# A chunked recurrence's output made by channel: two heads on two column halves, three full channel tiles, and masked products that alternate between row halves

## The chip, the cores and the metric

One core of a Trainium2 chip. Times are device microseconds of one launch, the median of three or more runs. All arithmetic is float32. In the profile of this kernel a float32 product is two instructions on TensorE (PE): RV's eight products in each of 24 chunks count 384. So "x16" is eight products.

## The reference, cut to what matters

```python
batch, n_heads, seq, head_dim = (4, 8, 768, 40)
for t in range(S):
    y[:, :, t] = np.einsum('bhd,bhde->bhe', rt, state)
    Sa = np.einsum('bhde,bhe->bhd', state, at)
    state_decay = state * wt[:, :, None, :] - np.einsum('bhd,bhe->bhde', Sa, bt)
    state = state_decay + np.einsum('bhd,bhe->bhde', vt, kt)
# ... y as (batch * seq, 320), then
h = np.maximum(x @ w_in, 0.0)          # w_in 320 x 2048
return (h * h @ w_out)                 # w_out 2048 x 320
```

## The kernel before

The recurrence runs in chunks of 128 steps: 4 batches with 6 chunks each are 24 chunks. Within a chunk the eight heads go in four pairs. A head has 40 channels, padded to 64, so a pair fills 128 partitions. Everything that depends on the state is a handful of products per head; the inverse of a triangular matrix (six levels of products and transposes) takes the largest part of TensorE's time (27.5 of 70.3 us in a regular chunk, by start-to-start distances). After every two chunks the second part, the squared-relu network, gets 256 tokens. Its blocks of six `w_in` or eight `w_out` instructions are issued between the stages of the recurrence, so that TensorE has work while DVE or ACT empties PSUM (below: evicts a block).

Four places matter. The masked products, one row half (parity of the head) after the other:

```python
def products(name, bufs, l_, r_):
    res = []
    for e in range(2):
        p_ = quads(psum(ps_w))
        rows = slice(e * DP, e * DP + D)
        for q in range(NP):
            mm(p_[:, q], l_[rows, q, :], r_[rows, q, :], True)
        # ... DVE multiplies by the triangular mask
```

They make N, A, RV and RX: 4 x 24 = 96 blocks of 16 instructions. The output of a chunk, by token, with 40 streamed columns for each head:

```python
heads(y_, g["RV"], lambda h: k_[:, h, :D], True)
for q in range(NP):
    mm(y_[:, 2 * q:2 * q + 2], rT[:, q], sd[:, q, :, :D], False)
heads(y_, rx, lambda h: b_[:, h, :D], False)
nc.vector.tensor_tensor(ys, y_, g["wn"], Alu.mult)     # wn: the decays, turned back to tokens
```

The turning of the tokens to channels, and the second part, whose 320 channels are tiles of 128, 128 and 64 rows:

```python
for j, (o, m_) in enumerate(KT):
    nc.tensor.transpose(p_[:m_, j * C:(j + 1) * C], ys[:, o:o + m_], ident)
# ... copies by ACT, then
for j, (_, m_) in enumerate(KT):
    mm(p_, w_in[:m_, j, f * 128:(f + 1) * 128], t_[:m_, j, :], j == 0)
```

Of the kernel before, what the change touches and what calls it, by code (L numbers as in the profile page):

```python
# [17 lines left out]
def kernel(  # L18
# [11 lines left out]
):  # L30
    # The recurrence runs in chunks of C steps.  Within a chunk, with E_j the product of the decays
    # of the steps before j and all products taken relative to the middle of the chunk:
    #   a' = a E_t, k' = k / E_t+1, b' = b / E_t+1           (per key channel)
    #   N = strictly lower (a' b'^T), A = strictly lower (a' k'^T)
    #   x = (I + N)^-1 (a' S^T + A v)                         (the rows S a of all steps)
    #   y = E_t (r S + low(r v^T) k' - low(r x^T) b')
    #   S <- E_C (S + v^T k' - x^T b')
    # (I + N)^-1 is exact: the inverses of its diagonal blocks, doubled in size level by level.
    # Heads go in pairs, 64 partitions or columns each; tiles by head are [., parity, pair, .].
    nc = tc.nc  # L40
# [10 lines left out]
    GB = 2  # L51
    KT = [(o, min(128, DM - o)) for o in range(0, DM, 128)]

# [13 lines left out]
    def single(name, shape):  # L67
        return const.tile(shape, FP32, tag=name, name=name)
# [5 lines left out]

# [1 line left out]
    class Ring:  # L76
# [19 lines left out]
    def load(i):  # L96
        bb, c = order[i]
        loaded[i] = {}
        for nm, ring in rings.items():
# [4 lines left out]

# [1 line left out]
    ident = single("ident", [128, 128])  # L106
# [6 lines left out]
                            pattern=[[1, 128]], channel_multiplier=-1)  # L113
    # -1 at [2p, 2p + 1]: the first level, transposed.
    first = single("first", [128, 128])
# [4 lines left out]
                            pattern=[[-2, 64]], channel_multiplier=1)  # L120
    # -1 where the row is in the second and the column in the first half of one block of 2 n.
    halves = {}
    for lv in range(1, LEVELS):
# [9 lines left out]
                                pattern=[[2 * n, count], [0, n]], channel_multiplier=-1)  # L133
    # 1 where a state's row and column belong to the same head of a pair.
    same = single("same", [128, NP, 2])
# [7 lines left out]

    w_in = single("w_in", [128, len(KT), DFF])
    w_out = single("w_out", [128, NF, DM])

    # Weights come as float64 in raw words: the chip rounds them to float32.  hi holds the sign, 11 bits
    # of exponent and 20 of mantissa, lo the 32 bits below.  With p = sign and power of two, from hi:
    # weight = (p with hi's mantissa) + p lo 2^-52, the sum rounded once.
    def rounded(dst, src, n):  # L150
        raw = work.tile([128, WP, 2], I32, tag="raw", name="raw")[:n, :dst.shape[-1]]
        nc.scalar.dma_start(out=raw.rearrange("p f e -> p (f e)"), in_=src.bitcast(I32))
        lo, hi = raw[:, :, 0].bitcast(U32), raw[:, :, 1]
        power = work.tile([128, WP], I32, tag="power", name="power", bufs=1)[:n, :dst.shape[-1]]
        p_ = work.tile([128, WP], I32, tag="signed", name="signed", bufs=1)[:n, :dst.shape[-1]]
        bits = dst.bitcast(I32)
        nc.vector.tensor_scalar(power, hi, 20, 0x7FF, Alu.logical_shift_right, Alu.bitwise_and)
        nc.vector.tensor_scalar(power, power, 896.0, 1151.0, Alu.max, Alu.min)
        nc.vector.tensor_scalar(power, power, 896.0, float(1 << 23), Alu.subtract, Alu.mult)
        nc.vector.tensor_scalar(p_, hi, -(1 << 31), None, Alu.bitwise_and)  # L160
        nc.vector.tensor_tensor(p_, p_, power, Alu.bitwise_or)  # L161
        nc.vector.tensor_scalar(bits, hi, 0xFFFFF, 3, Alu.bitwise_and, Alu.logical_shift_left)
        nc.vector.tensor_tensor(bits, bits, p_, Alu.bitwise_or)  # L163
        rest = power.bitcast(FP32)
        nc.vector.scalar_tensor_tensor(rest, lo, 2.0 ** -52, p_.bitcast(FP32), Alu.mult, Alu.mult)  # L165
        nc.vector.tensor_tensor(dst, dst, rest, Alu.add)

    WP = 320
    WI = 256
    pieces = [(w_in[:n, j, f:f + WI], moe_w_in[o:o + n, f:f + WI], n)  # L170
              for f in range(0, DFF, WI) for j, (o, n) in enumerate(KT)]
    pieces += [(w_out[:, f, :], moe_w_out[f * 128:(f + 1) * 128, :], 128) for f in range(NF)]

    def load_weights(n):
        for _ in range(min(n, len(pieces))):
            dst, src, rows = pieces.pop(0)
            if src.dtype == FP32:
                nc.scalar.dma_start(out=dst, in_=src)
            else:
                rounded(dst, src, rows)  # L180

# [1 line left out]
    def turn(x_):  # L183
# [5 lines left out]
    def products(name, bufs, l_, r_):  # L189
        """Strictly upper part of l_^T r_ by head, as one tile a parity."""  # L190
        res = []
        for e in range(2):
            p_ = quads(psum(ps_w))
            rows = slice(e * DP, e * DP + D)
            for q in range(NP):
                mm(p_[:, q], l_[rows, q, :], r_[rows, q, :], True)
            t_ = work.tile([128, NP, 128], FP32, tag=name, name=name, bufs=bufs)
            nc.vector.tensor_tensor(t_, p_, over4(upper), Alu.mult)  # L198
            res.append(t_)
        return res  # L200

    def inverse(g):
        """(I + N)^-1 transposed, from N transposed: both parities in step, a stage at a time."""
        new = lambda nm, bufs: work.tile([128, NP, 128], FP32, tag=nm, name=nm, bufs=bufs)
# [38 lines left out]
    def decay(i, g):  # L243
        """Products of the decays, and N, which the inverse waits for."""
        x_ = loaded[i]
# [18 lines left out]
    def rest(i, g):  # L264
        """What the chain needs beside the inverse."""
        x_ = loaded.pop(i)
        up, down, aT = g["dec"][:, 0], g["dec"][:, 1], g["aT"]
        kT, rT, vT = turned("kT", 1), turned("rT", 2), turned("vT", 1)
# [16 lines left out]

        wn = g["wn"] = work.tile([128, H, D], FP32, tag="wn", name="wn")
        nc.scalar.copy(wn, back(up[:, :, :C]))
        yield
        inv = back(down[:, :, 1:C + 1])
# [5 lines left out]

# [1 line left out]
    ended, tokens = {}, {}  # L297

    def chain(i, g):
# [53 lines left out]
        yield  # L353
        y_ = by_head(psum(ps_c))
        heads(y_, g["RV"], lambda h: k_[:, h, :D], True)
        if c > 0:
            for q in range(NP):
                mm(y_[:, 2 * q:2 * q + 2], rT[:, q], sd[:, q, :, :D], False)
        heads(y_, rx, lambda h: b_[:, h, :D], False)
        ys = work.tile([128, H, D], FP32, tag="ys", name="ys")  # L360
        nc.vector.tensor_tensor(ys, y_, g["wn"], Alu.mult)  # L361
        yield
        gather(i, ys.rearrange("t h d -> t (h d)"))
        yield

# [1 line left out]
    def gather(i, ys):  # L367
        """Tokens of GB chunks by channel, for the second part."""
        n = i % GB
        if n == 0:  # L370
            tokens[i // GB] = work.tile([128, len(KT), GB * C], FP32, tag="tokens", name="tokens")
        t_ = tokens[i // GB]
        p_ = psum(ps_c)
        for j, (o, m_) in enumerate(KT):
            nc.tensor.transpose(p_[:m_, j * C:(j + 1) * C], ys[:, o:o + m_], ident)  # L375
        full = sum(m_ == 128 for _, m_ in KT)
        nc.scalar.copy(t_[:, :full, n * C:(n + 1) * C], p_[:, :full * C].rearrange("p (j t) -> p j t", j=full))
        for j in range(full, len(KT)):
            m_ = KT[j][1]
            nc.scalar.copy(t_[:m_, j, n * C:(n + 1) * C], p_[:m_, j * C:(j + 1) * C])  # L380

    PART = NF // 4

    def ffn():
        for gi in range(len(order) // GB):
# [4 lines left out]
            for f in range(NF):  # L390
                p_ = psum(ps_f)[:, :GB * C]
                for j, (_, m_) in enumerate(KT):
                    mm(p_, w_in[:m_, j, f * 128:(f + 1) * 128], t_[:m_, j, :], j == 0)
                h_ = work.tile([128, GB * C], FP32, tag="hid", name="hid", bufs=NF + 2)
                nc.scalar.activation(h_, p_, Act.Relu)  # L395
                nc.vector.tensor_tensor(h_, h_, h_, Alu.mult)  # L396
                hid.append(h_)
                yield True
# [12 lines left out]

    # ---- in the order that the engines take it: while one stage's result leaves PSUM, the tensor
# [1 line left out]
    second = ffn()  # L414
# [70 lines left out]
```

## Time and profile before

| | before |
|---|---|
| median of three runs (lowest, highest) | 1795.6 us (1790.55, 1799.59) |
| mean granted clock of TensorE, profiled run | 0.970 |
| start of the fifth chunk (weights unpacked, second part running) | 293.8 us |
| regular chunk at full clock | 70.29 us |
| last chunk and the second part after it | 151.8 us |

The last three are read from the starts of TensorE's instructions: a chunk starts with the transpose of its `w`. Chunks alternate between 72.3 and 68.3 us, because every second one has more of the second part; 70.29 is the mean of twelve.

This is the table of windows again, cut where the stages change (columns: window, length, busy us of PE, PEld (its weight loads), DVE, ACT, POOL, then clock, DMA share, GB/s):

```profile
0.00:294.00 294.00, 237.11 (x1663) 214.88 (x1664) 233.69 (x584) 45.03 (x88) 12.25 (x61) 0.88 0.28 57
294.00:1644.00 1350.00, 1349.64 (x9899) 1179.93 (x9897) 694.50 (x1246) 263.10 (x566) 0.00 (x0) 0.99 0.09 17
```

TensorE is busy in 99.97% of the 1350 us of steady chunks, yet its clock there is 0.99 and not 1.00.

### The profile page before, as it was taken

To read this page: it belongs to the slowest core of one execution; us is meant where nothing else is said; L and a number is where in the kernel's file an instruction comes from. 1 tells how busy PE (TensorE), PEld (TensorE's weight loads), DVE (VectorE), ACT (ScalarE), POOL (GpSimd) and SP (SyncE) were. 2 spreads that over 40 slices of the span, in tenths; PEclk is the share of its full clock that TensorE was granted. 3 is DMA by queue.
4 is the path that set the end of the run, shared out by engine and by line. 5 is a ranking of instruction groups with operands and counts; after the bars stand their busy time and mean duration, and the time that the engine had idled before them with its cause. 6 is when DMAs were issued, how large, how long until landed. Compare 5 with 4: busy or idle time off the path is not lost.

```text
span 1795.3 us, 29170 instructions
## 1 busy us (share of the span) xinstructions
PE 1734.9 (97%) x12408; PEld 1509.1 (84%) x12408; DVE 976.8 (54%) x1921; ACT 335.0 (19%) x717; POOL 12.2 (1%) x61
## 2 busy tenths in 40 slices
PE   4886999999999999999999999999999999999999
PEld 4776888888888888888888888888888888888875
DVE  7989866355455554545645545635635544545411
ACT  0111222112112112212212212212212211211211
POOL 2000000000000000000000000000000000000000
PEclk9868899999999999999999999999999999989999
DMA  7213110010110100100101101001001011000000
GB/s 107 57 50 81 52 23 12 16 26 5 19 23 12 19 20 12 23 16 16 23 12 20 23 12 19 12 16 26 12 16 26 9 19 23 5 1 8 1 8 8
DMA packets 158593, 39.88 MB, mean 22 GB/s; under 512 B 150784, under 2 KB 153856, under 8 KB 158464
## 3 DMA queue, kind: packets, MB, share of 16 engines
q1 hardware_dynamic: 153216, 27.54, 8.9%
q10 hardware_dynamic: 5248, 10.49, 2.0%
q8 instruction: 98, 1.61, 0.4%
q14 instruction: 31, 0.25, 0.0%
HBM read 34.08 MB, written 3.93 MB: 21 GB/s over the span
## 4 chain that ended last, share of the span: by engine, by line
PE 92%; DVE 6%; DMA 2%; issue 0%; ACT 0%; DVEq 0%; ACTq 0%
PE ps_w L65 37%; PE ps_f L65 28%; PE ps_c L65 13%; PE ps_w L217 7%; PE ps_w L186 4%; DMA raw<-in_moe_w_in_dram 1%; PE ps_w L283 1%; PE ps_c L338 1%; PE ps_c L327 1%; PE ps_c L375 1%; DVE power L165 1%; DVE signed L161 0%; DVE inv L237 0%; DVE inv_g L226 0%; DMA raw<-in_moe_w_out_dram 0%; DVE w_in L163 0%
## 5 line engine op out<-in xcount | busy, mean ns | idle before, releaser
L226 DVE TENSOR_TENSOR inv_g<-ps_w,half 128x512 f32<-128x512 f32 x288 | 198.9, 691 | 272.8 <-PE ps_w L65 272.6
L65 PE MATMUL ps_f<-tokens,w_in 128*128 128x256 f32 (+1 forms) x1152 | 323.3, 400 | 0.0
L65 PE MATMUL ps_w<-inv,N 128*128 128x128 f32 x2304 | 298.3, 285 | 0.0
L65 PEld LDWEIGHTS ps_w<-inv,N 128*128 128x128 f32 x2304 | 282.5, 200 | 8.4 <-issue 4.7
L65 PEld LDWEIGHTS ps_f<-tokens,w_in 128*128 128x128 f32 (+1 forms) x1152 | 187.0, 189 | 79.2 <-issue 69.2
L65 PE MATMUL ps_w<-inv_g,inv_t 128*128 128x128 f32 x1920 | 242.0, 279 | 4.8 <-DVE inv_g L226 4.7
L65 PEld LDWEIGHTS ps_w<-inv_g,inv_t 128*128 128x128 f32 x1920 | 228.4, 193 | 19.8 <-issue 12.0
L237 DVE TENSOR_TENSOR inv<-ps_w,inv 128x512 f32<-128x512 f32 x240 | 165.5, 690 | 123.4 <-PE ps_w L65 120.4
L65 PE MATMUL ps_f<-w_out,hid 128*128 128x320 f32 x768 | 220.5, 433 | 0.0
L218 ACT COPY inv_t<-ps_w 128x512 f32<-128x512 f32 x240 | 130.4, 588 | 387.8 <-PE ps_w L217 378.4
L396 DVE TENSOR_TENSOR hid<-hid 128x256 f32<-128x256 f32 x192 | 81.4, 424 | 217.3 <-ACT hid L395 217.3
L65 PEld LDWEIGHTS ps_f<-w_out,hid 128*128 128x128 f32 x768 | 139.6, 190 | 48.5 <-issue 0.7
L395 ACT ACTIVATE hid<-ps_f 128x256 f32<-128x256 f32 x192 | 73.8, 384 | 388.5 <-PE ps_f L65 388.5
L217 PE MATMUL ps_w<-ident,inv 128*128 128x128 f32 x960 | 131.6, 278 | 8.0 <-DVE inv L237 7.8
L217 PEld LDWEIGHTS ps_w<-ident,inv 128*128 128x128 f32 x960 | 106.3, 141 | 37.4 <-issue 13.9
L65 PE MATMUL ps_w<-aT,bT 40*128 40x128 f32 x384 | 43.2, 299 | 25.7 <-DVE aT L258 25.7
L65 PEld LDWEIGHTS ps_w<-aT,bT 40*128 40x128 f32 x384 | 41.8, 205 | 27.9 <-DVE aT L258 26.4
L361 DVE TENSOR_TENSOR ys<-ps_c,wn 128x320 f32<-128x320 f32 x24 | 11.8, 492 | 82.9 <-PE ps_c L65 82.9
L65 PE MATMUL ps_c<-in_b,RX 128*128 128x40 f32 x384 | 52.7, 300 | 1.2 <-DVE RX L198 1.1
L65 PEld LDWEIGHTS ps_c<-in_b,RX 128*128 128x128 f32 x384 | 51.0, 212 | 2.3 <-DVE RX L198 2.2
L65 PEld LDWEIGHTS ps_w<-inv_t,inv_g 128*128 128x128 f32 x384 | 45.6, 192 | 6.3 <-issue 4.4
L237 DVE TENSOR_TENSOR inv_t<-ps_w,inv_t 128x512 f32<-128x512 f32 x48 | 33.2, 691 | 32.1 <-PE ps_w L65 32.1
(115 smaller groups left out, 1802.8 us busy)
## 6 DMA issues: line engine op xcount, KB each, us to landing
raw<-in_moe_w_out_dram ACTq DMA_DIRECT2D x16, 320.0 KB, 2.9
raw<-in_moe_w_in_dram ACTq DMA_DIRECT2D x16, 256.0 KB, 2.7
in_w<-in_w_dram SPq DMA_DIRECT2D x24, 160.0 KB, 2.7
in_a<-in_a_dram SPq DMA_DIRECT2D x24, 160.0 KB, 2.7
in_k<-in_k_dram SPq DMA_DIRECT2D x24, 160.0 KB, 2.7
in_b<-in_b_dram SPq DMA_DIRECT2D x24, 160.0 KB, 3.1
in_r<-in_r_dram SPq DMA_DIRECT2D x24, 160.0 KB, 3.4
in_v<-in_v_dram SPq DMA_DIRECT2D x24, 160.0 KB, 2.7
```

The source lines that it names most:

```text
L65: nc.tensor.matmul(o, l_, r_, start=start, stop=True, skip_group_check=True)
L165: nc.vector.scalar_tensor_tensor(rest, lo, 2.0 ** -52, p_.bitcast(FP32), Alu.mult, Alu.mult)
L186: nc.tensor.transpose(p_[:, q * 128:(q + 1) * 128], pair(x_, q), ident)
L217: nc.tensor.transpose(p_[:, q], src[e][:, q], ident)
L218: nc.scalar.copy(dst[e], p_)
L226: nc.vector.tensor_tensor(gs[e], p_, over4(halves[lv]), Alu.mult)
L237: nc.vector.tensor_tensor(to, p_, to, Alu.add)
L283: nc.tensor.transpose(p_[:, q * 128:(q + 1) * 128], d_[:, q], ident)
L327: nc.tensor.transpose(p_[:, q * 128:(q + 1) * 128], st[:, q].rearrange("p e d -> p (e d)"), ident)
L338: nc.tensor.transpose(p_[:, q * 128:(q + 1) * 128], pair(xn, q), ident)
L395: nc.scalar.activation(h_, p_, Act.Relu)
L396: nc.vector.tensor_tensor(h_, h_, h_, Alu.mult)
```

## The change

The intent: make y with channels on partitions. Then it needs no transposes before the second part, the decays needn't be turned back, two heads are meant to run on the two column halves of the array, and the second part can have three full tiles of 128 channels. The seventh and eighth heads go, in pieces, into the gaps that padding leaves between the others, by four small transfers a chunk for the tokens and by more loads for the weights. Besides, the masked products alternate between the two row halves. The core of the diff:

```diff
 def products(name, bufs, l_, r_):
+        ps = [quads(psum(ps_w)) for _ in range(2)]
+        for q in range(NP):
+            for e in range(2):
+                rows = slice(e * DP, e * DP + D)
+                mm(ps[e][:, q], l_[rows, q, :], r_[rows, q, :], True)
# ... (the mask by DVE as before)
-        wn = g["wn"] = work.tile([128, H, D], FP32, tag="wn", name="wn")
-        nc.scalar.copy(wn, back(up[:, :, :C]))
# ...
-        heads(y_, g["RV"], lambda h: k_[:, h, :D], True)
+        y_ = quads(psum(ps_c))
         if c > 0:
             for q in range(NP):
-                mm(y_[:, 2 * q:2 * q + 2], rT[:, q], sd[:, q, :, :D], False)
-        heads(y_, rx, lambda h: b_[:, h, :D], False)
+                mm(y_[:, q], sd[:, q].rearrange("p e d -> p (e d)"), rT[:, q], q == 0)
+        for m_, rows in ((g["RV"], k_), (rx, b_)):
+            for q in range(NP):
+                for e in range(2):
+                    mm(y_[e * DP:(e + 1) * DP, q], rows[:, 2 * q + e, :], m_[e][:, q], c == 0 and q == 0 and rows is k_)
# ... (the transposes and copies of the tokens removed)
+        nc.vector.tensor_tensor(t_, y_, g["dec"][:, 0, :, :C], Alu.mult)
+        for j, row, h, d, m_ in gaps:
+            at = (h % 2) * DP + d
+            nc.sync.dma_start(out=t_[row:row + m_, j], in_=t_[at:at + m_, NT])
# ...
-                for j, (_, m_) in enumerate(KT):
-                    mm(p_, w_in[:m_, j, f * 128:(f + 1) * 128], t_[:m_, j, :], j == 0)
+                for j in range(NT):
+                    mm(p_, w_in[:, j, f * 128:(f + 1) * 128], t_[:, j, :], j == 0)
# ... weights: each piece of w_in zeroed by POOL, then loaded in several transfers
+        if sum(m_ for _, m_, _ in srcs) < n:
+            nc.gpsimd.memset(raw, 0)
+        for row, m_, src in srcs:
+            nc.scalar.dma_start(out=raw[row:row + m_].rearrange("p f e -> p (f e)"), in_=src.bitcast(I32))
```

More of the change, by code (lines that the diff above doesn't have):

```diff
@@ L51 @@
     GB = 2
-    KT = [(o, min(128, DM - o)) for o in range(0, DM, 128)]
+    NT = NP - 1
+    HALF = DP - D
+    gaps = []
+    for e in range(2):
+        h = 2 * NT + e
+        gaps += [(e, D, h, 0, HALF), (e, DP + D, h, HALF, D - HALF)]
+    places = [(h // 2, (h % 2) * DP, h * D, D) for h in range(2 * NT)]
+    places += [(j, row, h * D + d, n) for j, row, h, d, n in gaps]
     const = ctx.enter_context(tc.tile_pool(name="const", bufs=1))
@@ L142, with rounded @@
     states = Ring("state", B, [128, NP, 2, DP], 0.0, lambda t_: t_)
-    w_in = single("w_in", [128, len(KT), DFF])
+    w_in = single("w_in", [128, NT, DFF])
     w_out = single("w_out", [128, NF, DM])
-    def rounded(dst, src, n):
-        raw = work.tile([128, WP, 2], I32, tag="raw", name="raw")[:n, :dst.shape[-1]]
-        nc.scalar.dma_start(out=raw.rearrange("p f e -> p (f e)"), in_=src.bitcast(I32))
+    def rounded(dst, srcs):
+        raw = work.tile([128, WP, 2], I32, tag="raw", name="raw")[:, :dst.shape[-1]]
+        n = 128
+        if sum(m_ for _, m_, _ in srcs) < n:
+            nc.gpsimd.memset(raw, 0)
+        for row, m_, src in srcs:
+            nc.scalar.dma_start(out=raw[row:row + m_].rearrange("p f e -> p (f e)"), in_=src.bitcast(I32))
         lo, hi = raw[:, :, 0].bitcast(U32), raw[:, :, 1]
@@ L169 @@
     WI = 256
-    pieces = [(w_in[:n, j, f:f + WI], moe_w_in[o:o + n, f:f + WI], n)
-              for f in range(0, DFF, WI) for j, (o, n) in enumerate(KT)]
-    pieces += [(w_out[:, f, :], moe_w_out[f * 128:(f + 1) * 128, :], 128) for f in range(NF)]
+    pieces = [(w_in[:, j, f:f + WI], [(row, n, moe_w_in[o:o + n, f:f + WI]) for j_, row, o, n in places if j_ == j])
+              for f in range(0, DFF, WI) for j in range(NT)]
+    pieces += [(w_out[:, f, :], [(0, 128, moe_w_out[f * 128:(f + 1) * 128, :])]) for f in range(NF)]
     def load_weights(n):
         for _ in range(min(n, len(pieces))):
-            dst, src, rows = pieces.pop(0)
-            if src.dtype == FP32:
-                nc.scalar.dma_start(out=dst, in_=src)
-            else:
-                rounded(dst, src, rows)
+            dst, srcs = pieces.pop(0)
+            if moe_w_in.dtype != FP32:
+                rounded(dst, srcs)
+                continue
+            if sum(m_ for _, m_, _ in srcs) < 128:
+                nc.gpsimd.memset(dst, 0.0)
+            for row, m_, src in srcs:
+                nc.scalar.dma_start(out=dst[row:row + m_], in_=src)
     def turn(x_):
@@ L189, in products @@
     def products(name, bufs, l_, r_):
-        res = []
-        for e in range(2):
-            p_ = quads(psum(ps_w))
-            rows = slice(e * DP, e * DP + D)
-            for q in range(NP):
-                mm(p_[:, q], l_[rows, q, :], r_[rows, q, :], True)
+        ps = [quads(psum(ps_w)) for _ in range(2)]
[3 more added lines that the diff above has]
+                mm(ps[e][:, q], l_[rows, q, :], r_[rows, q, :], True)
+        res = []
+        for p_ in ps:
             t_ = work.tile([128, NP, 128], FP32, tag=name, name=name, bufs=bufs)
@@ L266, in rest @@
         x_ = loaded.pop(i)
-        up, down, aT = g["dec"][:, 0], g["dec"][:, 1], g["aT"]
+        down, aT = g["dec"][:, 1], g["aT"]
         kT, rT, vT = turned("kT", 1), turned("rT", 2), turned("vT", 1)
@@ L284, in back @@
             return p_.rearrange("t (h d) -> t h d", h=H)[:, :, :D]
-        wn = g["wn"] = work.tile([128, H, D], FP32, tag="wn", name="wn")
-        nc.scalar.copy(wn, back(up[:, :, :C]))
-        yield
         inv = back(down[:, :, 1:C + 1])
@@ L353, in chain @@
         yield
-        y_ = by_head(psum(ps_c))
-        heads(y_, g["RV"], lambda h: k_[:, h, :D], True)
+        y_ = quads(psum(ps_c))
         if c > 0:
             for q in range(NP):
-                mm(y_[:, 2 * q:2 * q + 2], rT[:, q], sd[:, q, :, :D], False)
-        heads(y_, rx, lambda h: b_[:, h, :D], False)
-        ys = work.tile([128, H, D], FP32, tag="ys", name="ys")
-        nc.vector.tensor_tensor(ys, y_, g["wn"], Alu.mult)
-        yield
-        gather(i, ys.rearrange("t h d -> t (h d)"))
-        yield
-    def gather(i, ys):
+                mm(y_[:, q], sd[:, q].rearrange("p e d -> p (e d)"), rT[:, q], q == 0)
+        for m_, rows in ((g["RV"], k_), (rx, b_)):
+            for q in range(NP):
+                for e in range(2):
+                    mm(y_[e * DP:(e + 1) * DP, q], rows[:, 2 * q + e, :], m_[e][:, q], c == 0 and q == 0 and rows is k_)
         n = i % GB
         if n == 0:
-            tokens[i // GB] = work.tile([128, len(KT), GB * C], FP32, tag="tokens", name="tokens")
-        t_ = tokens[i // GB]
-        p_ = psum(ps_c)
-        for j, (o, m_) in enumerate(KT):
-            nc.tensor.transpose(p_[:m_, j * C:(j + 1) * C], ys[:, o:o + m_], ident)
-        full = sum(m_ == 128 for _, m_ in KT)
-        nc.scalar.copy(t_[:, :full, n * C:(n + 1) * C], p_[:, :full * C].rearrange("p (j t) -> p j t", j=full))
-        for j in range(full, len(KT)):
-            m_ = KT[j][1]
-            nc.scalar.copy(t_[:m_, j, n * C:(n + 1) * C], p_[:m_, j * C:(j + 1) * C])
+            tokens[i // GB] = work.tile([128, NP, GB * C], FP32, tag="tokens", name="tokens")
+        t_ = tokens[i // GB][:, :, n * C:(n + 1) * C]
+        nc.vector.tensor_tensor(t_, y_, g["dec"][:, 0, :, :C], Alu.mult)
+        for j, row, h, d, m_ in gaps:
+            at = (h % 2) * DP + d
+            nc.sync.dma_start(out=t_[row:row + m_, j], in_=t_[at:at + m_, NT])
+        yield
     PART = NF // 4
```

## The prediction

> **What bounds the kernel now.** I read the page's busy shares first, then the table of windows, then the chain of waits, and then the tensor engine's timeline of one steady chunk (two chunks of 128 steps make one group of the second part).
>
> ```profile
> PE 1734.9 (97%) x12408; PEld 1509.1 (84%) x12408; DVE 976.8 (54%) x1921; ACT 335.0 (19%) x717; POOL 12.2 (1%) x61
> PE 92%; DVE 6%; DMA 2%; issue 0%; ACT 0%; DVEq 0%; ACTq 0%
> ```
>
> The first line says PE is never without work; the second, that the chain which ended last runs through PE for 92% of the span. Waits on DVE and DMA (8%) are where the weights are unpacked, at the start:
>
> ```profile
> 0.00:45.00 45.00, 22.24 (x127) 19.70 (x128) 33.77 (x87) 4.46 (x7) 12.25 (x61) 1.00 0.78 107
> 45.00:90.00 45.00, 36.63 (x276) 34.26 (x274) 40.60 (x117) 6.62 (x13) 0.00 (x0) 0.89 0.22 58
> 1000.00:1045.00 45.00, 45.00 (x355) 40.04 (x355) 25.72 (x49) 9.11 (x20) 0.00 (x0) 1.00 0.13 23
> ```
>
> Columns: window, its length, then busy us of PE, PEld, DVE, ACT, POOL, then clock, DMA share, GB/s. At 0 to 90 us DVE is the fuller engine; at 1000 us PE is full and DVE 57%. So from about 180 us to the end a PE microsecond removed is a microsecond of time, until a wait takes its place.
>
> "Busy" hides what PE spends it on, as one matmul takes 270 to 430 ns from start to end while the next starts 110 ns later. I therefore use start-to-start distances of the timeline (start, length, engine, line, what, shapes, count). Every float32 product is two instructions.
>
> ```profile
> 1011.65 1.74 PE L65 MATMUL ps_f<-tokens,w_in 128*128 128x256 f32 x6
> 1013.23 1.61 PE L65 MATMUL ps_w<-aT,bT 40*128 40x128 f32 x16
> 1014.77 0.66 PE L338 MATMUL ps_c<-ident,minus_x 128*128 128x128 f32 x4
> ...
> 1016.84 1.12 PE L65 MATMUL ps_c<-in_v,in_k 128*128 128x80 f32 x8
> 1017.80 1.06 PE L65 MATMUL ps_c<-minus_x,in_b 128*128 128x80 f32 x8
> 1018.69 0.60 PE L186 MATMUL ps_w<-ident,in_k 128*128 128x128 f32 x4
> ...
> 1021.42 0.27 PE L65 MATMUL ps_w<-aT,kT 40*128 40x128 f32 x1
> 1021.42 0.27 PE L65 MATMUL ps_w<-rT,xnT 40*128 40x128 f32 x1
> ...
> 1024.73 1.88 PE L65 MATMUL ps_c<-in_k,RV 128*128 128x40 f32 x16
> 1026.44 1.10 PE L65 MATMUL ps_c<-sd,rT 128*128 128x80 f32 x8
> 1027.37 1.92 PE L65 MATMUL ps_c<-in_b,RX 128*128 128x40 f32 x16
> 1029.12 0.64 PE L186 MATMUL ps_w<-ident,in_r 128*128 128x128 f32 x4
> ...
> 1039.25 2.32 PE L65 MATMUL ps_f<-w_out,hid 128*128 128x320 f32 x8
> 1041.41 1.04 PE L217 MATMUL ps_w<-ident,inv 128*128 128x128 f32 x8
> ```
>
> Three readings. First, w_out takes (1041.41 - 1039.25)/8 = 0.270 us for 320 columns, so 0.216 for 256. Six w_in instructions should take 1.30 us; they take 13.23 - 11.65 = 1.58. Two of the six have only 64 rows (the third channel tile), and the changes of row shape cost the 0.28. The block after such a change is longer too: in_v,in_k takes 0.96, its twin minus_x,in_b 0.89. Second, in_k,RV takes 1.71/16 = 0.107 for a mere 40 columns[...]. Third, two 40-row products start at the same 1021.42: two row halves do run side by side in float32, but only where one half's tail meets the other's head, as the kernel issues all four products of one half and then those of the other.
>
> [...]about 0.36 us per 64-row visit (0.28 plus 0.07 to 0.10 in the block after), 0.18 per change. [...]The trace shows side-by-side rows, and no column tiles at all: for float32 columns no run here speaks.[...]
>
> **The change, part by part.** I counted changes of array shape in the built order of PE's instructions, which is almost the same chunk by chunk.
>
> (a) Channel tiles. 320 channels as 128+128+64 become three tiles of 128 rows, with the seventh and eighth heads in the gaps between the others. The 192 visits to 64 rows vanish. Changes into or out of a row shape: 476 before, 142 after; 334 x 0.18 = 60 us. New changes into or out of 64 columns are 58 against 48 cheap ones before (the 64-row transpose of ys was entered without a pause); I charge 4. Saved: 56.
>
> (b) Alternating halves. 96 blocks of 16. Alone a block takes 1.54 (1013.23 to 1014.77), of which 0.19 is the change of shape, so 1.35; two in a row take 2.74, so 1.27 each without it. With the halves alternating, eight slots of 0.111 plus one to lead in are 1.0. Saved: 0.3 x 96 = 29.
>
> (c) Transposes. By channel, y needs no turning of tokens (3 per chunk) and no decay turned back for it (4 per chunk): 168 x 0.109 = 18. The ACT copies go as well (wn, tokens: 0.44, 0.37 and 0.26 us a chunk), but ACT is at 19%.
>
> (d) Output products. RV and RX take 1.71 + 1.75 = 3.46. In the new form the masked product streams 128 columns past 64 weight columns; an instruction still takes 0.108[...]. If the two column halves run side by side, 17 slots are 1.85 and a chunk saves 1.6, 39 us in 24 chunks. If they don't, 32 slots are 3.46 and nothing is saved. sd stays at 8 instructions[...]. I give side by side 70%: 27.
>
> (e) What is added. DVE's product for y grows from 320 to 512 columns (0.49 to 0.69 us, 5 us in all, off the path). Four small transfers per chunk carry the two last heads into the gaps. Loads here land after 2.7 to 3.4 us, but the first w_in matmul that needs them stands some 10 us of PE work later; hidden, except after the last chunk (about +2). Weight loads go from 24 to 80 transfers, each some 0.33 us of ACT's queue (18 us in the first 150), and each piece is zeroed by POOL beforehand (0.53 us). Against this, DVE's order now puts the first chunk's decays ahead of unpacking: in the trace before, PE waited 12.5 us for aT at 24 us. I put the start at 0, give or take 10.
>
> Sum: 56 + 29 + 18 + 27 = 130.
>
> Losses: the first two chunks are DVE's, so 2/24 of (b), (c), (d), 6. New waits, since the same DVE work now hides behind less PE work: inv_t was ready 0.54 us early in the steady chunks (gap between its last DVE operation and the transpose) and loses 0.7 of cover, the 0.3 of (b) among it; both RV evictions now start late, and the next block needs their banks; the first inverse level loses a decay transpose that stood between two blocks whose eviction is ready only 0.1 us early. About 0.2 + 0.35 + 0.2 a chunk, 16 in 22 chunks. With the 2 of the tail: 24. Net 106: about 1690 us; with side-by-side columns 1678, without about 1708. I predict 1685.
>
> **Rivals.** One: column halves don't overlap. [...]for it, that float32 goes as two passes with their own weight loads, and that no column tiles appear in the trace. Then 1700 to 1715. Two: DVE becomes the bound. It has 57% in the steady window and gains 0.2 us a chunk while the chunk shrinks 6%, so 61%: too little for a bound, but its latency makes waits; were these 2 us a chunk rather than 0.75, 1715. Three: the start. If the 56 extra transfers hold up ACT's copies of the inverse, DVE and PE idle together, and the first 180 us may become 195. Four: the new waits don't come, since the issue order moves work into them: 1662.
>
> **Range and chances.** The four drive the range: 1655 to 1718 us. Two per cent faster is below 1759.7 us; the sum without columns and with doubled waits still lies below it, and (a), (b) and (c) rest on distances measured here. Faster 0.96, within 2% 0.035, slower 0.005.
>
> **What would show it.** (a): six w_in instructions in 1.30 us, all of 128 rows. (b): a lone block of 16 from 1.54 to about 1.2 with its change of shape, pairs starting within some ns of each other. (c): no ys or wn groups, half of the decay transposes. (d): RV,in_k and RX,in_b, 32 instructions in about 1.9 us (side by side) or 3.5. New waits: PE behind inv_t, RV or inv_g, adding to some 16 us, where now there is next to nothing after the start. The first 180 us should hold about the same work. The prediction is wrong [...]if w_in still takes 1.58, or if the tokens' transfers show up as a PE wait in each group.

## The result, and the profile after

The changed kernel took 1622.11 us (median of four runs, 1620.61 to 1624.85), with correct results. That lies 33 us below the predicted range. The ratio is 0.904, 95% interval 0.902 to 0.906. Ratios here are the mean time of one kernel's fast runs over that of the other's in the same rounds, so not quite the ratio of the quoted medians.

```profile
PE 1550.1 (96%) x12240; PEld 1399.5 (86%) x12240; DVE 971.6 (60%) x1921; ACT 315.8 (19%) x645; POOL 24.2 (1%) x85
PE 87%; DVE 6%; DMA 1%; issue 0%; ACT 0%; DVEq 0%; ACTq 0%
```

From the page: TensorE still has work 96% of the time, with 168 instructions fewer, all of them transposes. DVE's busy time has hardly changed (976.8 to 971.6 us), so its share grew to 60%. In the window 1000 to 1045 us it is 60% too, where the prediction said 61%; it is not the bound. The windows, cut at the same stages (fifth chunk, last chunk):

```profile
0.00:274.00 274.00, 209.30 (x1665) 188.29 (x1666) 231.60 (x586) 42.86 (x81) 24.16 (x85) 0.92 0.31 61
274.00:1486.00 1212.00, 1210.69 (x9731) 1099.93 (x9730) 690.57 (x1244) 247.24 (x506) 0.00 (x0) 1.00 0.10 19
```

Almost the same number of instructions (9731 against 9899) fits into 1212 instead of 1350 us, and the clock of the stretch is 1.00. Here is TensorE's timeline of the same part of a steady chunk as in the prediction (L65 before and L74 after are the helper `mm`):

```profile
1041.59 1.46 PE L74 MATMUL ps_f<-tokens,w_in 128*128 128x256 f32 x6
1042.88 0.60 PE L203 MATMUL ps_w<-ident,in_b 128*128 128x128 f32 x4
...
1046.93 1.16 PE L74 MATMUL ps_w<-aT,bT 40*128 40x128 f32 x16
1048.03 0.66 PE L353 MATMUL ps_c<-ident,minus_x 128*128 128x128 f32 x4
...
1057.14 0.83 PE L74 MATMUL ps_c<-rT,sd 128*128 128x128 f32 x6
1057.90 1.09 PE L74 MATMUL ps_c<-RV,in_k 128*64 128x128 f32 x16
1058.83 1.04 PE L74 MATMUL ps_c<-RX,in_b 128*64 128x128 f32 x16
1059.80 0.66 PE L203 MATMUL ps_w<-ident,in_r 128*128 128x128 f32 x4
```

Six `w_in` instructions take 1042.88 - 1041.59 = 1.29 us where they took 1.58. The masked block aT,bT takes 1.10 where it took 1.54. RV and RX take 1059.80 - 1057.90 = 1.90 where they took 3.46: here the column halves do run side by side in float32 (experiment 3: RX takes 0.97 us on two halves and 1.85 on one).

Where did the 175.7 us between the two profiled runs (1795.3 and 1619.6) go? I summed, for each group of instructions, the distance from each matmul's start to the next one's. The three stretches are those of the windows:

| stretch | before | after | difference |
|---|---|---|---|
| to the start of the fifth chunk | 293.8 | 274.2 | -19.6 |
| the next 19 chunks | 1349.7 | 1212.1 | -137.6 |
| last chunk and the rest of the second part | 151.8 | 133.2 | -18.6 |

Of the middle row, 19 x 6.29 = 119.5 us are what a regular chunk at full clock became shorter (70.29 to 64.00). About 18 us are left over; that remainder turns out to be clock, which the experiments take up. The last row is mostly 32 blocks of `w_in` at 0.32 us less each, 10.4 us. Inside the regular chunk:

| in a regular chunk, us | before | after | difference |
|---|---|---|---|
| eight `w_in` blocks | 12.71 | 10.59 | -2.12 |
| four masked blocks | 5.93 | 4.25 | -1.68 |
| RV and RX products | 3.45 | 1.90 | -1.55 |
| decay transposes and token transposes | 1.29 | 0.44 | -0.86 |
| waiting ahead of a level's inv,N | | | +0.16 |

The rest, some -0.2, is spread over blocks that follow a removed change of array shape (in_v,in_k went from 0.96 to 0.85 us, in_b's transposes from 0.49 to 0.44), less a little for sd (0.93 to 0.99), whose instructions now stream 128 columns instead of 80.

### The profile page after: what moved, and what is told of

Its sections match the earlier page's. It is cut to its first block, busy times and chain, and to the rows that moved or that the text cites. A ratio compares the mean times of both kernels' runs of the same rounds, so it can differ in the third digit from the quotient of the medians.

```text
span 1619.6 us, 29073 instructions
## 1 busy us (share of the span) xinstructions
PE 1550.1 (96%) x12240; PEld 1399.5 (86%) x12240; DVE 971.6 (60%) x1921; ACT 315.8 (19%) x645; POOL 24.2 (1%) x85
## 3 DMA queue, kind: packets, MB, share of 16 engines
q1 hardware_dynamic: 156480, 28.52, 10.2%
## 4 chain that ended last, share of the span: by engine, by line
PE 87%; DVE 6%; DMA 1%; issue 0%; ACT 0%; DVEq 0%; ACTq 0%
PE ps_w L74 35%; PE ps_f L74 27%; PE ps_c L74 12%; PE ps_w L235 7%; PE ps_w L203 4%; DMA raw<-in_moe_w_out_dram 1%; PE ps_c L353 1%; DVE inv L255 1%; PE ps_w L301 1%; PE ps_c L342 1%; DVE inv_t L227 0%; DVE N L216 0%; DVE signed L175 0%; DVE power L179 0%; DVE inv_g L244 0%; DVE inv_t L228 0%
## 5 line engine op out<-in xcount | busy, mean ns | idle before, releaser
L74 PE MATMUL ps_w<-inv,N 128*128 128x128 f32 x2304 | 287.4, 278 | 0.3 <-DVE RV L216 0.3
L74 PE MATMUL ps_f<-tokens,w_in 128*128 128x256 f32 x1152 | 282.2, 382 | 0.0
L74 PEld LDWEIGHTS ps_w<-inv,N 128*128 128x128 f32 x2304 | 272.7, 193 | 6.6 <-DVE RV L216 0.5
L74 PE MATMUL ps_w<-inv_g,inv_t 128*128 128x128 f32 x1920 | 239.5, 277 | 4.7 <-DVE inv_g L244 4.5
L74 PEld LDWEIGHTS ps_w<-inv_g,inv_t 128*128 128x128 f32 x1920 | 227.7, 192 | 18.0 <-issue 5.6
L74 PEld LDWEIGHTS ps_f<-tokens,w_in 128*128 128x128 f32 x1152 | 204.7, 191 | 20.8 <-issue 0.5
L74 PE MATMUL ps_f<-w_out,hid 128*128 128x320 f32 x768 | 220.9, 433 | 0.0
L74 PEld LDWEIGHTS ps_f<-w_out,hid 128*128 128x128 f32 x768 | 139.6, 190 | 47.6 <-issue 0.2
L235 PEld LDWEIGHTS ps_w<-ident,inv 128*128 128x128 f32 x960 | 109.6, 141 | 26.2 <-DVE inv L255 10.2
L235 PE MATMUL ps_w<-ident,inv_t 128*128 128x128 f32 x192 | 31.9, 294 | 25.3 <-DVE inv_t L228 22.1
L235 PEld LDWEIGHTS ps_w<-ident,inv_t 128*128 128x128 f32 x192 | 23.6, 151 | 29.9 <-issue 24.4
L74 PEld LDWEIGHTS ps_w<-inv_t,inv_g 128*128 128x128 f32 x384 | 46.4, 192 | 3.3 <-issue 0.7
L236 ACT COPY inv<-ps_w 128x512 f32<-128x512 f32 x48 | 28.1, 586 | 105.1 <-PE ps_w L235 85.6
L74 PEld LDWEIGHTS ps_w<-aT,bT 40*128 40x128 f32 x384 | 25.7, 204 | 26.1 <-DVE aT L276 19.1
L74 PE MATMUL ps_w<-aT,bT 40*128 40x128 f32 x384 | 30.6, 304 | 18.2 <-DVE aT L276 18.2
```

The costliest lines, as they stand in the source:

```text
L74: nc.tensor.matmul(o, l_, r_, start=start, stop=True, skip_group_check=True)
L235: nc.tensor.transpose(p_[:, q], src[e][:, q], ident)
L236: nc.scalar.copy(dst[e], p_)
```

## The experiments

Twelve kernels ran. "Before" and "after" say which kernel an edit was made to. Unless noted, each gave the reference's results. A figure in us against the kernel before is the difference of medians in the same rounds; the ratio is to the kernel before. The changed kernel was timed in the first rounds alone, so a figure against it crosses rounds, between which the median of the kernel before moved from 1790 to 1796 us; for these the lengths of chunks in the traces are the firmer evidence.

### 1. The full third tile alone

The kernel before, with the third tile's missing 64 rows filled by zeros, so that all `w_in` products have 128 rows; heads stay where they were, and y is still made by token.

```diff
+    nc.gpsimd.memset(w_in[64:, len(KT) - 1, :], 0.0)
+    tok_ring = Ring("tokens", 2, [128, len(KT), GB * C], 0.0, lambda t_: t_[64:, len(KT) - 1, :])
-                for j, (_, m_) in enumerate(KT):
-                    mm(p_, w_in[:m_, j, f * 128:(f + 1) * 128], t_[:m_, j, :], j == 0)
+                for j in range(len(KT)):
+                    mm(p_, w_in[:, j, f * 128:(f + 1) * 128], t_[:, j, :], j == 0)
```

> The kernel before with its third channel tile filled up to 128 rows with zeros (weights and tokens), nothing else changed; the order of the tensor engine's instructions is the same. Theory that the changes of array shape are paid in full: 338 of 490 row-shape changes go, at 0.18 us each, so 61 us less, about 1734 us, and six w_in instructions take 1.30 us. Rival, that waits for DVE and ACT take part of it back (my prediction's 'new waits'): 45 us or less, with new waits of PE in the steady chunks.

Measured: 1734.23 us, ratio 0.967 (0.9645 to 0.9697), clock 0.968. The gain is 61 us. A stretch of its timeline:

```profile
986.80 1.46 PE L65 MATMUL ps_f<-tokens,w_in 128*128 128x256 f32 x6
988.10 1.01 PE L65 MATMUL ps_c<-in_v,in_k 128*128 128x80 f32 x8
988.95 1.06 PE L65 MATMUL ps_c<-minus_x,in_b 128*128 128x80 f32 x8
```

The block takes 1.30 us although it now multiplies 64 rows of zeros, and the block after it 0.85 instead of 0.96. The added rows cost nothing here; what cost time was the change in the number of rows. With 338 changes of shape fewer in the built order, one is worth 61/338 = 0.18 us, as read off the timeline before. The clock has no part in this: a regular chunk at full clock went from 70.29 to 67.74 us, and 24 x 2.55 is 61, while the time at half clock was 109 us before and 113 here. A third of the whole gain has nothing to do with the recurrence, nor with packing heads into gaps: zero rows would have done.

### 2. Alternating halves alone, and undone

The first is the kernel before with the new `products`, the second the changed kernel with the old one.

```diff
# 2a, before:                          # 2b, after: the reverse
-        for e in range(2):
-            p_ = quads(psum(ps_w))
+        ps = [quads(psum(ps_w)) for _ in range(2)]
+        for q in range(NP):
+            for e in range(2):
```

> The kernel before with only the masked products alternating between the row halves. By the prediction's term, 0.3 us a block, 29 us less (1766). By what the two traces show in the steady chunks, 0.45 us a block, 43 us less (1752). If the earlier end of the first half's eviction mattered, less than 20 us.

> The changed kernel with the masked products again one row half after the other. Term of the prediction: 29 us more (1651). By the traces: 43 us more (1665). More than 43 if alternation also shortened waits that the faster tensor engine would otherwise meet.

Measured: alone 1737.24 us, ratio 0.968 (0.9666 to 0.9698); undone 1656.24, ratio 0.9225 (0.9209 to 0.9241). So the part is worth 58 us alone and 34 as the last part. The two don't contradict each other: a regular chunk shrinks by 1.84 us in the first (70.29 to 68.45) and by 1.71 in the second (65.71 to 64.00), which over 20 chunks is 37 and 34. The first four chunks give little: they end 6.4 us earlier in the first, about half of it clock, and only 0.3 us apart in the second. Most of the other 20 us of the first are spells at half clock, 37 us that the kernel before has after its fifth chunk's start and this one doesn't. Experiment 5 is about those.

### 3. Do column halves run side by side?

Two edits of the changed kernel. In one, all products of the first column half are issued before those of the second. In the other, both heads' RX products go to the lower half, which gives a wrong result but has the same instructions.

```diff
# 3a
-            for q in range(NP):
-                for e in range(2):
+            for e in range(2):
+                for q in range(NP):
# 3b
+                    to = 0 if rows is b_ else e * DP
-                    mm(y_[e * DP:(e + 1) * DP, q], rows[:, 2 * q + e, :], m_[e][:, q], ...)
+                    mm(y_[to:to + DP, q], rows[:, 2 * q + e, :], m_[e][:, q], ...)
```

> The changed kernel with the output products of one column half issued before those of the other. If columns run side by side only where neighbours in the order are of different halves, as the row halves did before, a pair of blocks takes 2.6 us rather than 1.9, so about 18 us more (1640). If the column halves overlap wherever they stand, no change (1622). If they don't overlap at all, 38 us more (1660).

> Wrong result on purpose: in the changed kernel both heads of a pair put their RX product on the lower column half, so that no two of these run side by side, in as many instructions of the same shape. If side by side is what the columns gain: the RX block goes from 0.97 to about 1.75 us a chunk, 19 us more (1641). If the gain came from the smaller weight load alone: no change (1622).

Measured: 1633.63 us for the first (+11.5 over the changed kernel) and 1640.72 for the second (+19). The timeline of the second, at the same place of a chunk:

```profile
1070.31 1.09 PE L74 MATMUL ps_c<-RV,in_k 128*64 128x128 f32 x16
1071.23 1.91 PE L74 MATMUL ps_c<-RX,in_b 128*64 128x128 f32 x16
1073.08 0.66 PE L203 MATMUL ps_w<-ident,in_r 128*128 128x128 f32 x4
```

RX on one half takes 1.85 us, on two 0.97 (RV, left on two halves, 0.92). 24 x 0.88 = 21 us, of which 19 showed up in the time. If RV gains as RX does (it was not tested alone), running side by side is worth twice that, some 38 us; the table above has 1.55 x 24 = 37.

The first edit fell between "all" and "nothing", and its timeline says why:

```profile
1064.84 1.25 PE L74 MATMUL ps_c<-RV,in_k 128*64 128x128 f32 x13
1065.83 0.32 PE L74 MATMUL ps_c<-RX,in_b 128*64 128x128 f32 x1
1065.93 0.27 PE L74 MATMUL ps_c<-RV,in_k 128*64 128x128 f32 x1
...
1066.21 1.20 PE L74 MATMUL ps_c<-RX,in_b 128*64 128x128 f32 x13
1067.34 0.66 PE L203 MATMUL ps_w<-ident,in_r 128*128 128x128 f32 x4
```

In the queue all sixteen RV instructions come before the first RX. Yet RX's first one, on the first column half, starts at 1065.83, ahead of three of RV's on the second, which start at 1065.93, 1066.04 and 1066.15. So here part of the overlap came without alternation (RV and RX in 2.50 us), and the rest of it with alternation (1.90).

### 4. The transposes, and the start

The changed kernel with the decays turned back and copied as before, though nobody reads them (4a). Then two runs on the start. The prediction had named two opposite effects: zeroing the pieces puts the first chunk's decays ahead of the unpacking in DVE's order, and more loads might hold up ACT's queue. The kernel before with the zeroing only (4b); the changed kernel with one load per piece and no zeroing, which loads wrong weights (4c).

```diff
# 4a, after
+        nc.scalar.copy(wn, back(g["dec"][:, 0, :, :C]))
# 4b, before
+        if dst.shape[-1] == WI:
+            nc.gpsimd.memset(raw, 0)
# 4c, after
+    pieces = [(d, [(0, 128, moe_w_in[j * 96:j * 96 + 128, f:f + WI])]) for ...]
```

> The changed kernel with the decay for y turned back to token order and copied out again, as before, though nothing reads it: four transposes and an ACT copy a chunk. At 0.109 us a transpose 10.5 us more (1632). If transposes hide behind waits, less than 4; if their slack was what kept later waits away (my prediction's 'the first inverse level loses a decay transpose'), also less than 10.5.

> The kernel before with POOL zeroing each w_in piece's buffer ahead of its load, which puts the first decays ahead of the unpacking in the vector engine's order, as in the changed kernel; all else as before. If this order is what shortened the first chunks: the second group's first w_in matmul and the third chunk start some 5 to 10 us earlier, 1785 to 1790 us. If the zeroing only adds a wait to each load: up to 10 us later, 1805.

> Wrong result on purpose: in the changed kernel each w_in piece comes as one transfer of 128 rows, without zeroing, instead of two or four with zeroing. If the 56 added transfers and the zeroing cost time at the start, 5 to 15 us less (1610 or so); if the vector engine sets the start anyway, within 4 us of 1622; if the order with the decays first is what helps and this loses it, up to 8 us more.

Measured: 4a 1630.45 us (+8): a regular chunk grew by 0.22 us, half of what the four transposes take (0.44); the other half lay in a wait that was there anyway, as the blocks around them, inv,N and inv_g,inv_t, became 0.14 and 0.07 us shorter. 4b 1783.97 (-10.7, ratio 0.9933 to 0.9977): the fifth chunk started at 291.8 instead of 293.8, with as much time at half clock before it, so the order of DVE's work is worth 2 us there. The rest is mostly fewer spells at half clock (20 instead of 41 us after the first 200). 4c 1628.81 (+7): the fifth chunk started at 278.1 instead of 274.2, with 65 instead of 44 us at half clock before it. The run without the 56 extra transfers is the slower one, but it also has 20 us more at half clock, worth up to 10 us; so a cost of the transfers of a few us is not ruled out. The changed kernel's start is earlier for its order and its clock together, and these runs don't split the two cleanly.

### 5. The clock

Every part so far had come out at its predicted size or somewhat over, and still some 25 us were unexplained. The trace holds the changes of TensorE's granted clock. In the kernel before, five spells at 0.50 fall after the fifth chunk's start, of 6.8, 6.8, 10.2, 10.2 and 3.4 us (37.4 together); in the first 294 us there are four, 71.6 us together. All are multiples of about 3.4 us. The changed kernel has two, both in the start (44.4 us). This is one of them in the kernel before, by windows and then by timeline:

```profile
1510.00:1517.00 7.00, 7.00 (x63) 6.59 (x61) 4.28 (x8) 1.52 (x4) 0.00 (x0) 1.00 0.05 10
1517.00:1527.00 10.00, 10.00 (x51) 9.66 (x51) 3.26 (x5) 0.53 (x2) 0.00 (x0) 0.51 0.15 27
```

```profile
1516.31 2.66 PE L65 MATMUL ps_c<-in_b,RX 128*128 128x40 f32 x16
1518.90 3.09 PE L65 MATMUL ps_w<-aT,kT 40*128 40x128 f32 x16
1521.92 3.78 PE L65 MATMUL ps_w<-inv,N 128*128 128x128 f32 x16
1525.50 0.85 PE L375 MATMUL ps_c<-ident,ys 128*128 128x128 f32 x3
```

PE is busy in all 10 us of the window, and does 51 instructions where 7 us beside it hold 63. inv,N takes 3.58 us; at full clock it takes 1.8 to 1.9. So TensorE slowed down without being idle. What precedes the spell is RV, sd and RX: 40 instructions in 4.39 us at full clock, which stream 32 x 40 + 8 x 80 = 1920 columns. With 0.84 ns a column (from `w_out`: 0.270 us for 320) the array streams, by this estimate, in 1.6 of 4.39 us, 37%, though "busy" throughout. The changed kernel streams 128 columns per instruction there. My theory: a low streaming share lets the clock fall. The rival: spells come by chance, or from idle times in the start. To test it alone, widen these products to the padded 64 columns per head, with the same number of instructions (5a): 32 x 64 + 8 x 128 = 3072 columns, 59% of the same stretch; and narrow RX to 8 columns per head (5b).

```diff
# 5a, before
-        heads(y_, g["RV"], lambda h: k_[:, h, :D], True)
+        heads(y_, g["RV"], lambda h: k_[:, h, :], True)
-                mm(y_[:, 2 * q:2 * q + 2], rT[:, q], sd[:, q, :, :D], False)
+                mm(y_[:, 2 * q:2 * q + 2], rT[:, q], sd[:, q, :, :], False)
-        heads(y_, rx, lambda h: b_[:, h, :D], False)
+        heads(y_, rx, lambda h: b_[:, h, :], False)
# 5b, before
+            mm(y_[:, h, :8], rx[h % 2][:, h // 2], b_[:, h, :8], False)
```

> The kernel before with the moving operand of the output products widened into the zero padding: 64 columns instead of 40 for RV and RX, 128 instead of 80 for sd. The instructions stay as many[...], so at full clock the time should not change. Theory that the granted clock halves after stretches in which the array is streamed through for too small a share: the half-clock spells of the steady part (41 us after the first 200 us in the profile before, 20 us lost) go or shrink, about 1775 us, and the mean clock rises from 0.970 to about 0.98. Rival, that the spells come from the row-half products or from chance: the spells stay, 1795 us.

> Wrong result on purpose: the kernel before with RX's products cut to 8 of the 40 columns; as many instructions[...]. The opposite of the widened run. If the granted clock halves after stretches of too small a streamed share: more and longer half-clock spells after the first 290 us than the 37 to 54 us that the kernel before and the padded one showed, and the time rises by 10 to 60 us. If the widened run lost its spells by chance: about as many spells, and a time within 5 us of 1795.

Measured: wider, 1778.52 us, ratio 0.992 (0.9906 to 0.9935), clock 0.983. That is within 2% of the kernel before, but the interval excludes 1: more work in the same instructions took 16 us less. Its regular chunk is 70.29 us, exactly that of the kernel before; no spell is left after the start; and its six runs lie within 2 us, where eleven of the kernel before lie within 12. Narrower, 1813.28 us, ratio 1.012 (1.0083 to 1.0156), clock 0.961: less work, 23 us more time, with 65 us at half clock after the first 290. At full clock RX's sixteen instructions take 1.75 us with 8 columns as with 40, and 1.73 with 64, so their own length does not explain either result. A window of the kernel before with a spell in it, and the same window of the wide one:

```profile
1496.00:1568.00 72.00, 72.00 (x504) 63.00 (x503) 38.23 (x69) 15.12 (x33) 0.00 (x0) 0.93 0.09 17
```

```profile
1496.00:1568.00 72.00, 72.00 (x543) 62.73 (x542) 41.12 (x78) 15.88 (x36) 0.00 (x0) 1.00 0.06 10
```

The number of instructions in 72 us, 504 against 543, differs by the clock: regular chunks are equally long. So here the width of these products moved the mean clock in both directions (0.970 as it was, 0.983 wider, 0.961 narrower); that is shown. What exactly trips a spell is shown only in part. In the kernel before (four spells of five) and in experiment 1 most steady spells follow a stretch of 37 to 38% streaming, but several such stretches have none after them. Experiment 2a, without a steady spell (clock 1.00 from 294 to 1600 us), is no counterexample: in its steady chunks the built order puts two of RV's eight products earlier, so its stretch is shorter (36 instructions in 3.94 us, from 1062.51 to 1066.45).

Within each run all changes of the clock lie on one grid of 3.413 us, to within 2 ns. For every grid interval at full clock after the fifth chunk's start, in all 14 traces, take the share in which columns stream (0.84 ns each, an estimate as above). Of the intervals under 37%, all in 5b, 7 of 7 were followed by a spell; from 37 to 38.6%, 12 of 22 (4 of 7 in the kernel before); from there to 45%, 1 of 25 (0 of 5 in the kernel before). The wide kernel has none below 48%, the changed kernel and its variants none below 52%. My reading of these counts, not tested by a run of its own, is that it matters whether a narrow stretch happens to fill a whole interval of the grid. The other six spells, all after 1590 us, followed intervals of 51 to 71% and stay unexplained.

### 6. A version that beats both

If y gains from column halves, so should x, whose products also stream 40 columns by 128 loaded ones. The changed kernel, with x made by channel too, and turned to tokens only where the state needs it (6a); and this with the weights unpacked one piece a round rather than two in the second chunk, to relieve DVE at the start (6b).

```diff
# 6a, after
-        heads(xs, g["TT"], lambda h: xr[:, h], True)
+        for q in range(NP):
+            for e in range(2):
+                mm(p_[e * DP:(e + 1) * DP, q], xr[:, 2 * q + e, :], g["TT"][e][:, q], q == 0)
+        nc.scalar.mul(xT, p_, -1.0)
+        if c < NCH - 1:
#            ... transposes of xT, copied to xn
# 6b, besides
-                load_weights(2)
+                load_weights(1)
```

> The same idea carried on: the rows x come by channel as well, from two heads on two column halves, and are turned to token order for the state alone (not at all in the last chunks). x falls from 1.71 us to about 0.93 plus 0.3 for two changes of shape, the four transposes stay at 0.44: about 0.5 us a chunk, 12 us less (1610). If the changes of shape cost as much as the rows', or the chain's next stage now waits for ACT's larger copy: no gain (1622).

> The kernel of the run before with the weights of the second part unpacked one piece a round in the second chunk too, rather than two. If the vector engine's crowding sets the length of the second and third chunk and the fourth has room: up to 8 us less than the run before. If the first w_in or w_out products then wait for their weights: up to 8 us more.

Measured: 6a 1607.97 us, ratio 0.897 (0.8942 to 0.9003), 14 us less than the changed kernel and the best of all; x's sixteen instructions take 1.03 instead of 1.70 us. 6b 1608.66: nothing gained, so the pace of unpacking in that chunk is not what the start waits for.

## Why the prediction was wrong

The direction, the bound and the mechanisms of (a) to (d) held; the saving came out 63 us too small (110.6 predicted, from 1795.6 to 1685; 173.5 measured). By its own steps:

**(a) Channel tiles**, 56 predicted. Experiment 1 gives 61. Right, and 0.18 us for a change of shape was the right price. Of the changes to 64 columns, the one into the third transpose of ys cost no visible pause in the kernel before (0.109 us from start to start, as between the full ones), as the prediction says; the one into the output products did in the changed kernel (0.205 us from sd's last start to RV's first, against 0.112 within sd).

**(b) Alternating halves**, 29 predicted, at 0.3 us a block. A block gave 0.42 (1.68/4), 34 us in all by experiment 2b. The eight slots were right; what was mis-sized is the "one to lead in". A lone block without its change of shape took 0.90 (1.09 - 0.19), which is eight slots of 0.112 and no ninth: 0.1 us in each of 96 blocks, less the first chunks.

**(c) Transposes**, 18 predicted. Experiment 4a gives 8 for the decays, and the token transposes 0.42 x 24 = 10. Right.

**(d) Output products**, 39 if side by side, entered at 70% as 27. They do run side by side; 38 by experiment 3b. The size was right; the weight cost 11 us. (A sum beside it was off: without column halves its terms give about 1715, not 1708. That had no part in the miss.) The only doubt was whether float32 products on two column halves overlap, which no trace of the kernel before could answer.

**Losses**, 24 predicted. This is the first step that failed: "both RV evictions now start late", "inv_t ... loses 0.7 of cover", "About 0.2 + 0.35 + 0.2 a chunk, 16 in 22 chunks" (cover: how long a result is ready before it is needed). The runs showed 0.16 us a chunk, some 4 us in all. One of the three waits did come: at the first level of the inverse, where a decay transpose is gone, PE lost these 0.16 us, and experiment 4a, which puts transposes back, hides half of them there. The other two did not. PE's list of waits between 280 and 1480 us (what is waited for, us in all, how many, the longest) has next to nothing:

```profile
PE ps_w L235 <- DVE inv_t L228: 0.7, 1, 0.7
PE ps_w L235 <- DVE RX L216: 0.5, 2, 0.3
```

For inv_t the loss of cover was right, and the wait that should follow from it was wrong. From the timelines of DVE and PE, first the kernel before, then the one after:

```profile
1017.79 0.69 DVE L210 TENSOR_TENSOR inv_t<-inv_t,ident 128x512 f32<-128x512 f32 x1
1019.13 1.04 PE L217 MATMUL ps_w<-ident,inv_t 128*128 128x128 f32 x8
```

```profile
1050.87 1.28 DVE L228 TENSOR_TENSOR inv_t<-inv_t,ident 128x512 f32<-128x512 f32 x2
1052.00 0.60 PE L235 MATMUL ps_w<-ident,inv_t 128*128 128x128 f32 x4
1052.43 0.39 PE L74 MATMUL ps_c<-rT,sd 128*128 128x128 f32 x2
1052.66 0.60 PE L235 MATMUL ps_w<-ident,inv_t 128*128 128x128 f32 x4
```

Before, the first transpose starts 1019.13 - 1018.48 = 0.65 us after DVE's last operation on inv_t has ended; after, it starts 0.15 us before that end (1052.00 against 1052.15). So 0.8 of cover went, and more than there was. Yet PE does not wait: the first four transposes need the first row half's inv_t alone, which was ready 0.45 us earlier, and the other four come 0.51 us after theirs was ready, as a product with sd now stands between them. I had measured the cover (0.54, to the transposes' first weight load) from the last operation to the first transpose, which does not need it, and did not see the order that the program would be built in. For RV, the evictions start no later: 1.19 us after the block's first matmul in both kernels (1033.42 - 1032.23 and 1063.80 - 1062.61). That the start would lose its share of (b) to (d), 6 us, was right in kind: those chunks gave little to 2a and 2b; but the figures of the experiments above already contain it. The 2 us of the tail did not come: PE's list of waits has none for the tokens' transfers, and from the last matmul to the end are 3.6 us in both kernels.

**What the sum lacked: the clock.** No step of the prediction has it. After the fifth chunk's start the kernel before spends 37 us at half clock, the changed one none: some 18 us of time. In the start, 71.6 us became 44.4, which is worth up to half of the difference, 14 us; the start as a whole came 20 us earlier, where 0 plus or minus 10 was predicted. That the wider output products are enough to clear the steady spells is shown by experiment 5a (no spell left after the start, 16 us less); the changed kernel with its row halves undone (2b) has none either, so it does not owe this to their alternation.

Together: 5 from (a), 5 from (b), 11 from (d) and 20 from losses turn the net of 106, which the prediction's items give, into 147. The 26 us that are left to 173 are what the clock can hold, 18 after the start and up to 14 in it; the share of the start is an estimate that no run separates. All errors have one sign, and the lower end of the range, 1655, lay only 7 us below the fourth rival alone. The fourth rival, "The new waits don't come, since the issue order moves work into them", was the one that came true, for inv_t with its reason, and its 1662 was still 40 us too high, for the clock, the full column halves and the mis-sized blocks.

## What to carry to other kernels

On an engine that is "97% busy", ask of each instruction what sets its length: here changes of array shape (0.18 us each), a pace of some 0.11 us an instruction however narrow its stream (8, 40 or 64 columns), and row or column halves that worked alone (a lone masked block took 1.54 us, with alternating row halves 1.10; RX 1.85 on one column half, 0.97 on two); all are visible in start-to-start distances and none in the busy share. Zero rows that keep one shape can be cheaper than exact ones (by 61 us here). Read the clock's column before predicting: a steady stretch at 0.99 held 18 us that no count of instructions finds, and widening narrow products with padding recovered 16 of them. Before predicting a new wait, find which operation the first waiting instruction needs, and look at the built order.
